# Second pair of k and q loaded in f32 on the hardware queues and turned sooner; last eviction in one copy

## The chip, the core and the metric

The kernel runs on one core of a Trainium2 chip. Its engines are TensorE (PE; its weight loads are listed as PEld), VectorE (DVE), ScalarE (ACT), GpSimd (POOL) and SyncE (SP). SyncE, ScalarE and GpSimd also issue DMA transfers; those of GpSimd can change the type on the way (f32 to bf16), those of SyncE and ScalarE here copy without a change of type. The metric is the device time of one execution in microseconds, and smaller is better.

## The reference

Two stages follow each other: attention with a soft cap on the scores, then a feed-forward layer whose hidden value is the larger of two products.

```
q, k, v: (8, 12, 448, 64) f32, cap = 30
scores = (q @ k^T) / 8
scores = cap * tanh(scores / cap)
attn   = softmax(scores)
x      = (attn @ v), heads side by side: (3584, 768)
out    = max(x @ w1, x @ w2) @ w_out        w1, w2: (768, 1024), w_out: (1024, 768)
```

The output has 3584 rows of 768 f32 values.

## The kernel before, in words

The heads are taken two at a time, as 48 pairs (`i`), and the pairs two at a time, as 24 units of four heads (`t`); a unit at a time goes through the attention (unit 2 is cut into two items of 256 and 192 queries, so the items `n` in the steps count to 25). The feed-forward layer is rewritten: `max(a, b) = relu(a - b) + b`, so that `out = relu(x (w1 - w2)) w_out + x (w2 w_out)`. The product `w2 w_out` is made once (`premultiply`), stage 1 makes `relu(x (w1 - w2))` and stage 2 sums both products into an output tile of 128 rows. All of this is cut into numbered groups of matmuls (140 of them), which run between the attention's matmuls.

The order is written out by hand, as the string `ORDER`: each step names a function and its arguments, and each engine executes its instructions in the order in which the steps give them. Nothing is rearranged later. The engines meet through semaphores: an instruction waits only for the data and the buffers that it needs. GpSimd's loads also share eight completion slots in turn, so a load waits for the one eight before it; the stores and loads of SyncE and ScalarE do the same among themselves.

The steps that matter here:

- `ld0 x` (`load_first`, L254): loads k or q of pair 0 in f32 into a tile of its own, k on SyncE's queue, q on ScalarE's. `cd x` (`cast_first`, L259) casts it to bf16 into `kqs`, k on VectorE, q on ScalarE.
- `lk i`, `lq i` (`load`, L272): k or q of pair i, cast on the way, on GpSimd's queue (L276). `lv`, `lw1`, `lw2`, `lwo` load v and the weights on the same queue.
- `dm`, `ms0`, `id`, `ms`: fill a dummy tile, the identity and the constants. `D bank n` (L331): n dummy matmuls of 128 columns that compute nothing that is used.
- `X i bank` (L356): 28 transposes on TensorE that turn k and q of pair i, of 64 by 64 each, into a PSUM bank; `Xh i c bank` does only k (c = 0) or only q (c = 1), 14 of them. `XC` (L366) copies them on VectorE to `qkT`.
- `S n s z` (L428): scores of part s of item n into PSUM slot z (0 or 1). `T n s` (L439): tanh on ScalarE, which reads the slot and so frees it. `L`, `TL` are the same for the last 64 keys (L448, L459). `E` (L463): the exponential on ScalarE.
- `W`, `WC`: turn w2 on TensorE and copy it. `O`, `M x y n`, `H`, `ev`: open a group, run n of its matmuls (L581; a single group in turn L576), hand the bank over, evict it. Groups 138 and 139 are the two column halves of the last output tile.

`stage2` (L632) evicts an output tile by half. For the last tile of the last batch it stores each half at once: the first half with one copy on VectorE (L650) and two stores, rows 0 to 63 on SyncE's queue (L651) and rows 64 to 127 on ScalarE's (L652); the second half with two copies, VectorE's for the first 64 rows (L655) and ScalarE's for the others (L656), which writes into the f32 tile that had held k of pair 0 (`kr` in the profile), and then the two stores (L657, L658).

The first steps are, in the order before:

```
ld0 q; dm; ms0; D 0 32; cd q; ld0 k; cd k; lq 3 0; id; Xh 0 1 0; XC 0 1; Xh 0 0 1; XC 0 0; ms; S 0 2 0; T 0 2;
S 0 0 1; T 0 0; S 0 1 0; T 0 1; E 0 0 0 3; lk 1 0; lq 1 0; lq 2 0; X 1 2; XC 1; S 0 3 1; S 0 4 0; T 0 4; T 0 3;
E 0 1 0 2; lk 2 0; X 2 3; lk 3 0; lv 0 2; X 3 0; XC 2; D 1 8; XC 3; S 1 4 0; T 1 4; S 1 5 1; T 1 5; lw2 0; W 0 1;
```

Of the kernel before, what the change touches and what calls it, by code (L numbers as in the profile page):

```python
# [6 lines left out]


ORDER = """
ld0 q; dm; ms0; D 0 32; cd q; ld0 k; cd k; lq 3 0; id; Xh 0 1 0; XC 0 1; Xh 0 0 1; XC 0 0; ms; S 0 2 0; T 0 2;  # L10
S 0 0 1; T 0 0; S 0 1 0; T 0 1; E 0 0 0 3; lk 1 0; lq 1 0; lq 2 0; X 1 2; XC 1; S 0 3 1; S 0 4 0; T 0 4; T 0 3;
E 0 1 0 2; lk 2 0; X 2 3; lk 3 0; lv 0 2; X 3 0; XC 2; D 1 8; XC 3; S 1 4 0; T 1 4; S 1 5 1; T 1 5; lw2 0; W 0 1;
W 1 2; WC 1; L 0 0; TL 0; S 0 5 1; T 0 5; D 3 8; L 1 0; TL 1; WC 0; lwo 0 0; O 0 3; O 1 0; M 0 1 4; S 1 2 1; T 1 2;
lk 4 0; lwo 0 1; M 0 1 3; S 1 3 0; T 1 3; M 0 1 1; H 0; H 1; M 1 0 1; E 0 1 2 4; M 1 0 3; S 1 1 1; T 1 1; S 1 0 0;
# [149 lines left out]
def kernel(  # L164
# [11 lines left out]
    nc = tc.nc  # L176
    f32 = mybir.dt.float32
    bf16 = mybir.dt.bfloat16
# [3 lines left out]
    B, H, S, D = q.shape  # L182
    assert (H, S, D) == (12, 448, 64) and B % 2 == 0
    DM = H * D
    DF = moe_w1.shape[1]
    P = 128
    KC, FC = DM // P, DF // P
# [5 lines left out]
    VB = 4  # L193
    QB = 3
    NS = 3
    W2T = 6
    WOP = 2
    R7 = S // 64
    OB = 4
    CUT = 256  # L200
    SPLIT = (2,)
    scale = 1.0 / (D ** 0.5)

    ctx.enter_context(tc.manual_schedule())
    const = ctx.enter_context(tc.tile_pool(name="const", bufs=1))
    stage = ctx.enter_context(tc.tile_pool(name="stage", bufs=2))
    att = ctx.enter_context(tc.tile_pool(name="att", bufs=2))
# [13 lines left out]
    warm = const.tile([P, P], bf16, name="warm")  # L221
# [8 lines left out]
    def rows_of(i):  # L230
        return kqs[i // 2 % KB].rearrange("p j c -> p (j c)")[:, (i % 2) * 2 * S : (i % 2 + 1) * 2 * S]
# [19 lines left out]
    raw = {}  # L251
    SRC = {"k": k, "q": q, "v": v}

    def load_first(what):  # L254
        raw[what] = stage.tile([P, S], f32, name=what + "r", bufs=1)
        eng = nc.sync if what == "k" else nc.scalar
        eng.dma_start(out=raw[what], in_=rows7(SRC[what], 0))

    def cast_first(what):  # L259
        if what == "k":  # L260
            nc.vector.tensor_copy(rows_of(0)[:, :S], raw[what])
        else:
            nc.scalar.copy(rows_of(0)[:, S:], raw[what])

    def rows7(t, i):
        b, p = divmod(i, NP)
        return t[b, 2 * p : 2 * p + 2, :, :].rearrange("h (r j) d -> (h r) (j d)", j=R7)
# [77 lines left out]
    def keep_w2(c):  # L345
        w2T[c] = stage.tile([P, FC * P], bf16, name="w2T", bufs=W2T)
        nc.vector.tensor_copy(w2T[c], turned[c])
# [41 lines left out]
    def heads(t):  # L389
        return [divmod(m, 2) if turned_by_pe(t) else divmod(m, 2)[::-1] for m in range(4)]  # L390


    ITEMS = [
        (t, c0, w) for t in range(N // 2) for c0, w in (((0, CUT), (CUT, S - CUT)) if t in SPLIT else ((0, S),))
    ]

    def cut(n):
        return ITEMS[n][2] < S

    exps = {}  # L400
    slots = {}

    def exps_of(n, o):
        key = (n, 1 if cut(n) else o)
        if key not in exps:
            if key[1]:
                exps[key] = att.tile([P, 8 * S], bf16, name="e1")
            else:
                exps[key] = att.tile([P, 6 * S], bf16, name="e0")
        return exps[key]  # L410

    def e_of(n, o, h, j):
        w = ITEMS[n][2]
        if cut(n):
            x = 4 * (o if j < 2 else 2) + 2 * h + (j if j < 2 else o)
        else:
            x = 2 * j + h
        return exps_of(n, o)[:, x * w : (x + 1) * w]

    def left_of(n):  # L420
        w = ITEMS[n][2]
        b = 12 if cut(n) else 6
        return exps_of(n, 1)[:, b * w : (b + 2) * w].rearrange("p (o s) -> p o s", o=2)
# [15 lines left out]
    def tanh(n, s):  # L439
        w = ITEMS[n][2]  # L440
        if cut(n):
            e, m, x = exps_of(n, 1), 2 * w, s
        else:
            e, m, x = exps_of(n, s // NJ), w, s % NJ
        e = e[:, 2 * x * m : 2 * (x + 1) * m].rearrange("p (h s) -> p h s", h=2)
        nc.scalar.activation(e, slots[n, s][:, :, :m], AF.Tanh, scale=scale / cap)  # L446
# [42 lines left out]
    def total(n, bank):  # L489
        t, c0, w = ITEMS[n]  # L490
        ss = sums[n] = mm_tile(bank)
        HR = list(zip(heads(t), R32))
        if t < NS:
            for j in range(NJ):
# [108 lines left out]
    def stage1(b, f, c0, w):  # L603
        cs = slice((b % 2) * S + c0, (b % 2) * S + c0 + w)

        def unit(c):
            return wd_sb[:, c, f * P : (f + 1) * P], xT[b // 2][:, c, cs]

        def done(ps):
            if b // 2 not in gT:  # L610
                gT[b // 2] = xpool.tile([P, FC, 2 * S], bf16, name="gT", bufs=1)
            nc.vector.tensor_relu(gT[b // 2][:, f, cs], ps)  # L612

        return Group(KC, w, unit, done)
# [15 lines left out]
    osbs = {}  # L630

    def stage2(b, t, half):  # L632
        hs = slice(half * (DM // 2), (half + 1) * (DM // 2))
        ts = slice(t * P, (t + 1) * P)

        def unit(c):
            if c < KC:
                return xT[b // 2][:, c, ts], wm_sb[:, c, hs]
            return gT[b // 2][:, c - KC, ts], wo_sb[:, c - KC, hs]

        def done(ps):
            if (b, t) not in osbs:
                osbs[b, t] = osb_all[:, (7 * (b // 2) + t) % OB, :DM]
            o = osbs[b, t]
            if (b, t) != (B - 1, 6):
                nc.vector.tensor_copy(o[:, hs], ps)  # L646
                return
            to = out[b * S : (b + 1) * S, :].rearrange("(r j) n -> j r n", j=R7)[R7 - 2 :]
            if half == 0:
                nc.vector.tensor_copy(o[:, hs], ps)  # L650
                nc.sync.dma_start(out=to[0][:, hs], in_=o[:64, hs])  # L651
                nc.scalar.dma_start(out=to[1][:, hs], in_=o[64:, hs])  # L652
                return
            o2 = raw["k"][64:, : DM // 2]
            nc.vector.tensor_copy(o[:64, hs], ps[:64])  # L655
            nc.scalar.copy(o2, ps[64:])  # L656
            nc.sync.dma_start(out=to[0][:, hs], in_=o[:64, hs])  # L657
            nc.scalar.dma_start(out=to[1][:, hs], in_=o2)  # L658

        return Group(KC + FC, DM // 2, unit, done)  # L660

    groups = {}

    def number(new):
        for g in new:
            groups[len(groups)] = g

    number(premultiply(c, half) for half in range(2) for c in range(KC))
    for b in range(B):
        if b == 0 and SPLIT:  # L670
            number(stage1(b, f, 0, CUT) for f in range(FC))
            number(stage2(b, t, half) for t in range(CUT // P) for half in range(2))
            number(stage1(b, f, CUT, S - CUT) for f in range(FC))
            number(stage2(b, t, half) for t in range(CUT // P, 3) for half in range(2))
        else:
            number(stage1(b, f, 0, S) for f in range(FC))
            number(stage2(b, t, half) for t in (range(3) if b % 2 == 0 else range(3, 7)) for half in range(2))
# [4 lines left out]
    def moe(x, y, n):  # L682
# [6 lines left out]
                    groups[g].step(h)  # L689

    STEPS = {
        "ld0": load_first, "cd": cast_first, "ms": fill_const, "dm": lambda: nc.vector.memset(warm, 0.0),
        "ms0": lambda: nc.vector.memset(ident, 0.0), "id": identity, "D": keep_warm,
        "lk": lambda i, x: load("k", i, x), "lq": lambda i, x: load("q", i, x), "lv": load_v,
        "lw1": load_w1, "lw2": load_w2, "lwo": load_wo, "cr": cross,
# [45 lines left out]
```

## Time and profile before

| | |
|---|---|
| time, median of 3 runs | 329.57 us (329.55 to 329.63) |
| the profiled execution's own time | 329.6 us |
| its span in the profile | 327.8 us |
| TensorE busy | 318.9 us, 97% of the span |
| ScalarE busy | 273.8 us, 84% |
| VectorE busy | 244.8 us, 75% |
| GpSimd busy (mostly issuing loads) | 164.2 us, 50% |

A line of the timeline has the start in us, the busy time, the engine, the line of the kernel, the operation with output and input, the count, and in brackets how long the engine was idle before it and what it waited for. SPq and ACTq are the queues of SyncE and ScalarE as they issue transfers. The chain is the work that ended last, followed back from the last instruction to what released it. A busy TensorE is not TensorE at its peak: the ends of its matmuls are modelled.

### The profile page before, as it was taken

Reading aid. Unit: us, or ns where it says so; the run is one execution under the profiler, and the core shown is the slowest. Engines: PE = TensorE matmul, PEld = TensorE weight load, DVE = VectorE, ACT = ScalarE, POOL = GpSimd, SP = SyncE. Lnnn points to the kernel's source line nnn. Section 1 sums busy time; section 2 is a strip of 40 time slices with the busy share of each in tenths; the row PEclk is TensorE's granted clock in tenths of the full one; section 3 lists DMA queues with packets and bytes.
Section 4 is the critical chain, followed back from the end, with each engine's and each line's share of the span. In section 5 each row is a group of like instructions: output and inputs, shape, how many; then the busy total and the mean of one; then the engine's idle time right before and its main releaser. Section 6 shows DMA issues by size and latency. Waiting matters only on the chain.

```text
span 327.8 us, 10012 instructions
## 1 busy us (share of the span) xinstructions
PE 318.9 (97%) x4288; PEld 195.6 (60%) x4288; DVE 244.8 (75%) x446; ACT 273.8 (84%) x245; POOL 164.2 (50%) x243
## 2 busy tenths in 40 slices
PE   6899999999999999999999999999999999999994
PEld 5555567576556655655665565675567667655562
DVE  2339799889877887987888778878789775995421
ACT  4998999999999999999999998999899988710000
POOL 8447488988885994776567386543202000000000
PEclk9599999999999999999999999999999999999999
DMA  8999999999999999999999999995953042004006
GB/s 147 192 176 239 261 217 144 150 178 144 170 179 187 150 138 139 189 187 197 152 169 157 134 150 200 182 77 95 194 118 46 2 115 79 3 2 144 2 0 192
DMA packets 135083, 45.90 MB, mean 140 GB/s; under 512 B 116224, under 2 KB 130816, under 8 KB 134656
## 3 DMA queue, kind: packets, MB, share of 16 engines
q0 software_dynamic: 95456, 25.08, 75.8%
q1 hardware_dynamic: 39040, 19.18, 30.1%
q10 hardware_dynamic: 544, 1.02, 0.9%
q8 instruction: 33, 0.54, 0.7%
q14 instruction: 10, 0.08, 0.1%
HBM read 47.45 MB, written 11.01 MB: 178 GB/s over the span
## 4 chain that ended last, share of the span: by engine, by line
PE 88%; ACT 8%; DMA 1%; issue 1%; DVE 0%; DVEq 0%
PE mm L581 56%; PE s L538 8%; PE mm L576 8%; PE s L437 8%; ACT e L446 5%; ACT e L468 3%; PE s L528 2%; PE s L455 2%; PE mm L501 1%; DMA qr<-in_q_dram 1%; PE mm L364 1%; PE mm L496 1%; PE mm L343 1%; ACT e L461 0%; DVE qkT L369 0%
## 5 line engine op out<-in xcount | busy, mean ns | idle before, releaser
L468 ACT ACTIVATE e<-e 128x1792 bf16<-128x1792 bf16 (+4 forms) x73 | 140.7, 1937 | 0.3
L446 ACT ACTIVATE e<-s 128x896 bf16<-128x896 f32 (+2 forms) x144 | 123.8, 933 | 10.7 <-PE s L437 10.7
L581 PE MATMUL mm<-wo_sb,gT 64*128 64x384 bf16 x768 | 96.3, 323 | 0.0
L581 PE MATMUL mm<-xT,wd_sb 64*128 64x448 bf16 (+2 forms) x768 | 80.1, 326 | 0.0
L581 PE MATMUL mm<-wm_sb,xT 64*128 64x384 bf16 x576 | 77.2, 323 | 0.0
L283 POOL DMA_DIRECT2D kqs<-in_k_dram x76 | 54.5, 720 | 17.7 <-DMA kqs<-in_q_dram 7.7
L581 PEld LDWEIGHTS <-gT 64*128 64x128 bf16 x768 | 49.0, 94 | 22.6 <-issue 2.3
L581 PEld LDWEIGHTS <-wd_sb 64*128 64x128 bf16 x768 | 46.7, 94 | 19.8 <-issue 2.9
L437 PE MATMUL s<-qkT 64*128 64x448 bf16 (+2 forms) x300 | 53.9, 349 | 2.6 <-DVE qkT L369 1.3
L301 POOL DMA_DIRECT2D vp<-in_v_dram x48 | 30.4, 638 | 47.2 <-PE mm L501 28.2
L581 PEld LDWEIGHTS <-xT 64*128 64x128 bf16 x576 | 38.9, 94 | 16.6 <-issue 2.2
L612 DVE TENSOR_SCALAR gT<-mm 128x448 bf16<-128x448 f32 (+2 forms) x72 | 39.2, 567 | 10.2 <-PE mm L581 5.5
L646 DVE COPY osb<-mm 128x384 f32<-128x384 f32 x54 | 29.2, 552 | 19.3 <-PE mm L576 10.4
L283 POOL DMA_DIRECT2D kqs<-in_q_dram x38 | 34.9, 919 | 6.8 <-DMA kqs<-in_k_dram 3.9
L538 PE MATMUL s<-e,vp 128*32 128x448 bf16 (+2 forms) x600 | 32.5, 347 | 0.0
L557 DVE TENSOR_TENSOR xT<-s,inv 64x448 bf16<-64x448 f32 (+2 forms) x50 | 30.2, 603 | 2.2 <-PE mm L581 1.2
L301 POOL DMA_DIRECT2D vl<-in_v_dram x48 | 29.3, 619 | 4.0 <-DMA gT<-in_moe_w_dram 3.0
L437 PEld LDWEIGHTS <-qkT 64*128 64x128 bf16 x300 | 20.8, 94 | 17.4 <-issue 4.8
L656 ACT COPY kr<-mm 64x384 f32<-64x384 f32 x1 | 0.5, 473 | 36.0 <-DVE osb L655 36.0
L478 DVE TENSOR_TENSOR esum<-e 128x896 bf16<-128x896 bf16 x42 | 25.6, 616 | 5.0 <-PE mm L581 2.7
L483 DVE TENSOR_TENSOR esum<-esum,e 64x896 bf16<-64x896 bf16 x42 | 26.0, 618 | 3.1 <-PE mm L581 1.4
L478 DVE TENSOR_TENSOR esum<-esum,e 128x896 bf16<-128x896 bf16 x42 | 25.5, 622 | 3.1 <-PE mm L581 1.3
(56 smaller groups left out, 278.1 us busy)
## 6 DMA issues: line engine op xcount, KB each, us to landing
out_dram<-osb SPq DMA_DIRECT2D x51, 192.0 KB, 4.3
vp<-in_v_dram POOLq DMA_DIRECT2D x38, 160.0 KB, 5.1
kqs<-in_q_dram POOLq DMA_DIRECT2D x47, 112.0 KB, 5.5
kqs<-in_k_dram POOLq DMA_DIRECT2D x76, 56.0 KB, 4.8
osb<-in_moe_w_dram POOLq DMA_DIRECT2D x2, 1024.0 KB, 8.4
gT<-in_moe_w_dram POOLq DMA_DIRECT2D x3, 512.0 KB, 10.0
wo_sb<-in_moe_w_out_dram POOLq DMA_DIRECT2D x4, 384.0 KB, 8.6
w1l<-in_moe_w_dram POOLq DMA_DIRECT2D x1, 1024.0 KB, 6.1
```

The lines of the kernel that those rows point to most:

```text
L283: nc.gpsimd.dma_start(out=to, in_=x)
L301: nc.gpsimd.dma_start(out=to, in_=x)
L437: nc.tensor.matmul(ps[:, h, x * w : (x + 1) * w], k_of(t, o, h, j), q_of(n, o, h))
L446: nc.scalar.activation(e, slots[n, s][:, :, :m], AF.Tanh, scale=scale / cap)
L468: nc.scalar.activation(e[:, j0 * m : hi], e[:, j0 * m : hi], AF.Exp, scale=float(cap))
L478: nc.vector.tensor_add(d, e[:, 0:2, :] if j == 1 else d, e[:, 2 * j : 2 * j + 2, :])
L538: nc.tensor.matmul(vals[n][R32[m], u, :w], vp[t % VB][:, x, j if turned_by_pe(t) else 2 * j, u::2], e_of(n, o, h, j), start=False, stop=(j ...
L557: nc.vector.tensor_mul(x[to], vals[n][r, 1, :w], sums[n, 3][to, :w])
L576: nc.tensor.matmul(self.ps, w, x, start=first, stop=self.at[0] == self.n)
L581: ins = nc.tensor.matmul(self.ps, w[r], x[r], start=first, stop=self.at == [self.n, self.n]).ins
L612: nc.vector.tensor_relu(gT[b // 2][:, f, cs], ps)
L646: nc.vector.tensor_copy(o[:, hs], ps)
```

## The change

K and q of pair 1 are loaded as those of pair 0 were: in f32, k on SyncE's queue and q on ScalarE's, each behind pair 0's, and cast by VectorE (k) and ScalarE (q). GpSimd's queue has these two loads no more, and the loads behind them move up. Of pair 0, k is turned and copied before q, where it was q before k. The transposes of pair 1 move ahead of the third scores of item 0. In the last tile the second half is evicted as the first: one copy of 128 rows on VectorE, and two stores from the same tile. Three names are added that keep the sizes as they were: `EB = 2` (buffers of the exponentials, two before as well), `LASTW = 384` (columns of the last tile's first half, 384 before as well) and the width of a stage 2 group that follows from it.

```diff
 ORDER = """
-ld0 q; dm; ms0; D 0 32; cd q; ld0 k; cd k; lq 3 0; id; Xh 0 1 0; XC 0 1; Xh 0 0 1; XC 0 0; ms; S 0 2 0; T 0 2;
-S 0 0 1; T 0 0; S 0 1 0; T 0 1; E 0 0 0 3; lk 1 0; lq 1 0; lq 2 0; X 1 2; XC 1; S 0 3 1; S 0 4 0; T 0 4; T 0 3;
+ld0 k; ld0 q; ld1 k; ld1 q; dm; ms0; D 0 32; cd k; cd q; cd1 q; lq 3 0; id; Xh 0 0 1; XC 0 0; Xh 0 1 0; XC 0 1; cd1 k;
+ms; S 0 2 0; T 0 2; S 0 0 1; T 0 0; X 1 2; S 0 1 0; T 0 1; E 0 0 0 3; lq 2 0; XC 1; S 0 3 1; S 0 4 0; T 0 4; T 0 3;
...
-    def load_first(what):
-        raw[what] = stage.tile([P, S], f32, name=what + "r", bufs=1)
+    def load_first(what, i=0):
+        raw[what, i] = stage.tile([P, S], f32, name=f"{what}r{i}", bufs=1)
         eng = nc.sync if what == "k" else nc.scalar
-        eng.dma_start(out=raw[what], in_=rows7(SRC[what], 0))
+        eng.dma_start(out=raw[what, i], in_=rows7(SRC[what], i))
-    def cast_first(what):
+    def cast_first(what, i=0):
         if what == "k":
-            nc.vector.tensor_copy(rows_of(0)[:, :S], raw[what])
+            nc.vector.tensor_copy(rows_of(i)[:, :S], raw[what, i])
         else:
-            nc.scalar.copy(rows_of(0)[:, S:], raw[what])
+            nc.scalar.copy(rows_of(i)[:, S:], raw[what, i])
...
-                exps[key] = att.tile([P, 8 * S], bf16, name="e1")
+                exps[key] = att.tile([P, 8 * S], bf16, name="e1", bufs=EB)
...
-        hs = slice(half * (DM // 2), (half + 1) * (DM // 2))
+        w = LASTW if (b, t) == (B - 1, 6) else DM // 2
+        hs = slice(w, DM) if half else slice(0, w)
...
-            if half == 0:
-                nc.vector.tensor_copy(o[:, hs], ps)
-                nc.sync.dma_start(out=to[0][:, hs], in_=o[:64, hs])
-                nc.scalar.dma_start(out=to[1][:, hs], in_=o[64:, hs])
-                return
-            o2 = raw["k"][64:, : DM // 2]
-            nc.vector.tensor_copy(o[:64, hs], ps[:64])
-            nc.scalar.copy(o2, ps[64:])
+            nc.vector.tensor_copy(o[:, hs], ps)
             nc.sync.dma_start(out=to[0][:, hs], in_=o[:64, hs])
-            nc.scalar.dma_start(out=to[1][:, hs], in_=o2)
+            nc.scalar.dma_start(out=to[1][:, hs], in_=o[64:, hs])
...
+        "ld1": lambda w: load_first(w, 1), "cd1": lambda w: cast_first(w, 1),
```

More of the change, by code (lines that the diff above doesn't have):

```diff
@@ L195 @@
     NS = 3
+    EB = 2
     W2T = 6
@@ L201 @@
     SPLIT = (2,)
+    LASTW = 384
     scale = 1.0 / (D ** 0.5)
@@ L406, in exps_of @@
             if key[1]:
-                exps[key] = att.tile([P, 8 * S], bf16, name="e1")
+                exps[key] = att.tile([P, 8 * S], bf16, name="e1", bufs=EB)
             else:
-                exps[key] = att.tile([P, 6 * S], bf16, name="e0")
+                exps[key] = att.tile([P, 6 * S], bf16, name="e0", bufs=EB)
         return exps[key]
@@ L648, in done @@
             to = out[b * S : (b + 1) * S, :].rearrange("(r j) n -> j r n", j=R7)[R7 - 2 :]
-            if half == 0:
-                nc.vector.tensor_copy(o[:, hs], ps)
-                nc.sync.dma_start(out=to[0][:, hs], in_=o[:64, hs])
-                nc.scalar.dma_start(out=to[1][:, hs], in_=o[64:, hs])
-                return
-            o2 = raw["k"][64:, : DM // 2]
-            nc.vector.tensor_copy(o[:64, hs], ps[:64])
-            nc.scalar.copy(o2, ps[64:])
+            nc.vector.tensor_copy(o[:, hs], ps)
             nc.sync.dma_start(out=to[0][:, hs], in_=o[:64, hs])
-            nc.scalar.dma_start(out=to[1][:, hs], in_=o2)
-        return Group(KC + FC, DM // 2, unit, done)
+            nc.scalar.dma_start(out=to[1][:, hs], in_=o[64:, hs])
+        return Group(KC + FC, hs.stop - hs.start, unit, done)
     groups = {}
@@ L691 @@
     STEPS = {
-        "ld0": load_first, "cd": cast_first, "ms": fill_const, "dm": lambda: nc.vector.memset(warm, 0.0),
+        "ld0": load_first, "cd": cast_first, "ld1": lambda w: load_first(w, 1), "cd1": lambda w: cast_first(w, 1), "ms": fill_const, "dm": lambda: nc.vector.memset(warm, 0.0),
         "ms0": lambda: nc.vector.memset(ident, 0.0), "id": identity, "D": keep_warm,
```

## The prediction

> **What bounds the kernel now.** I read the page first, then the chain that ended last in order of time, then the timeline of the head and of the tail, then the clock by stretches. A row of the chain or the timeline gives start us, length us and what; a bracket gives the idle time before the row and what ended it.
>
> ```profile
> span 327.8 us, 10012 instructions
> ...
> PE 318.9 (97%) x4288; PEld 195.6 (60%) x4288; DVE 244.8 (75%) x446; ACT 273.8 (84%) x245; POOL 164.2 (50%) x243
> ...
> PEclk9599999999999999999999999999999999999999
> ...
> PE 88%; ACT 8%; DMA 1%; issue 1%; DVE 0%; DVEq 0%
> ```
>
> TensorE is the bound of the whole, with no slack to speak of, but the diff touches only the first 10 us and the last 5. There the chain is this:
>
> ```profile
> 0.74 3.56 DMA qr<-in_q_dram
> ...
> 4.33 0.57 ACT kqs L263
> ...
> 4.94 0.43 PE mm L364 x14
> ...
> 5.39 0.70 DVE qkT L369 x2
> ...
> 6.14 0.38 PE s L437 x2
> ...
> 6.54 2.54 ACT e L446 x3
> ...
> 14.89 1.62 ACT e L446 x2
> ...
> 16.55 0.37 PE s L437 x2
> 16.92 0.55 PE mm L335 x8
> ```
>
> Up to 6.54 us it is one string: q lands, ScalarE casts, TensorE turns q and k, VectorE copies both, the first scores, the first tanh (T 0 2). From 6.54 to 16.51 the chain stays on ScalarE without a gap, so TensorE's work in these 10 us is hidden. From 16.55 on it is TensorE's. So the head is worth what it moves the start of T 0 2, now 6.54. If TensorE falls behind before 16.55 it costs nothing, and after that everything.
>
> **The change part by part.** The head by its rows:
>
> ```profile
> 0.74 0.41 SPq L257 DMA_DIRECT2D kr<-in_k_dram  x1
> ...
> 1.17 1.28 ACT L263 ACT_TABLE_LOAD   x1 [1.17 <-PEq L722]
> 1.24 0.68 POOL L276 DMA_DIRECT2D kqs<-in_q_dram  x1 [0.79 <-POOLq L722]
> ...
> 2.79 1.09 POOL L276 DMA_DIRECT2D kqs<-in_q_dram  x2
> ...
> 4.16 0.47 DVE L261 CAST kqs<-kr 128x448 bf16<-128x448 f32 x1 [3.15 <-DMA kr<-in_k_dram]
> ...
> 4.94 0.63 PE L364 MATMUL mm<-ident,kqs 64*64 64x64 bf16 x28 [0.36 <-ACT kqs L263]
> ...
> 6.14 0.55 PE L437 MATMUL s<-qkT 64*128 64x448 bf16 x4 [0.57 <-DVE qkT L369]
> ...
> 7.51 0.37 PE L437 MATMUL s<-qkT 64*128 64x448 bf16 x2 [0.82 <-ACT e L446]
> ...
> 9.34 0.93 PE L437 MATMUL s<-qkT 64*128 64x448 bf16 x4 [0.73 <-DVE qkT L369]
> ```
>
> *K before q.* k's cast ends at 4.63, but its turning waits behind q's, whose cast ends at 4.90. In the new order k is turned from 4.67 (4.63 and the 0.04 seen between cast and turning). Its 14 transposes show at 5.10 (0.43), VectorE's copy runs 5.12 to 5.47 (half of 0.70). q is turned meanwhile, from about 4.99, its rows showing by 5.4, and its copy follows at 5.47 to 5.82. The first scores come at 5.87 instead of 6.14, and T 0 2 at 6.27 to 6.28: a gain of 0.26. q may land 0.1 later than now before this is touched.
>
> *The second issue on SyncE and ScalarE.* One costs 0.41. On ScalarE it pushes the table load from 1.17 to 1.57; that ends at 2.85, well before the cast at 4.33: nothing. SyncE has nothing else to do.
>
> *Two loads fewer on GpSimd's queue.* An issue is 0.55 (half of 1.09), so every later load is issued about 1.1 us sooner. The bytes read are the same. I price it at nothing, because TensorE waits for no transfer after the head; this is the whole list of what it waited for from 17 us to the end:
>
> ```profile
> PE mm L581 <- DVEq L589: 0.2, 1, 0.2
> ```
>
> *The casts of pair 1.* ScalarE's (the like one took 0.57) stands in front of T 0 2, VectorE's (0.47) behind the two copies. ScalarE is free from 4.90 to 6.28, so its cast costs nothing if q of pair 1 lands by 5.68. It costs the whole gain if it lands at 5.94, and beyond that each 0.1 costs 0.1. When it lands no row shows. These bound it:
>
> ```profile
> kr<-in_k_dram SPq DMA_DIRECT2D x1, 224.0 KB, 3.4
> qr<-in_q_dram ACTq DMA_DIRECT2D x1, 224.0 KB, 3.6
> ...
> 2.80:3.40 0.60, 1.00 1.06 409
> 3.40:4.40 1.00, 1.00 1.26 218
> ```
>
> (Landing in us after issue; then a stretch, its length, the clock, the share of the DMA engines, GB/s.) While the first pair's 458 KB moved, the engines gave 409 GB/s, so the second pair needs another 1.12 us behind q's landing at 4.30: 5.42 at the soonest. If GpSimd's transfers, the mixed 218 GB/s of the later stretch, take a third of the engines it is 4.30 + 1.68 = 5.98. Both ends stay in the range: a gain of 0.26, or a loss of 0.04. I take a landing of at most 5.68, since the 409 is nearer: the two hardware queues had the engines to themselves although GpSimd's first load was already issued at 1.24. The Trainium skill ("DMA: Bandwidth & Descriptors", Queues, rings and completion order) has each DMA engine go round between the queues that have work, a packet at a time. By that rule the third queue does take its third, the landing is 5.98 and the head is worth nothing; the row of 409 doesn't decide it, since it doesn't show when GpSimd's descriptors were ready.
>
> VectorE's cast delays the constants' fills (0.4) and the copy of pair 1's transposes. The constants are read only by the sums of the first unit, far behind. The copy now has no wait left that ScalarE would feel, as below.
>
> *Pair 1 turned sooner.* Its 28 transposes (0.63) move in front of the third scores, into the 0.82 in which TensorE waited for ScalarE: from 6.45 to 7.1, while the slot comes free at about 7.2. The wait of 0.73 at 9.34 goes. What is late next is ScalarE, which reads those scores only after the exponential that ends at 11.55. So nothing is gained, and nothing lost unless the k and q casts end after about 6.6.
>
> *The tail.* Column limits stay at 384 and the exponent buffers at two, so EB and LASTW change nothing. What changes is the last eviction:
>
> ```profile
> 323.63 0.55 DVE L655 COPY osb<-mm 64x384 f32<-64x384 f32 x1 [1.72 <-PE mm L576]
> 324.21 0.47 SPq L657 DMA_DIRECT2D out_dram<-osb  x1
> 324.22 0.47 ACT L656 COPY kr<-mm 64x384 f32<-64x384 f32 x1 [36.03 <-DVE osb L655]
> 324.72 0.47 ACTq L658 DMA_DIRECT2D out_dram<-kr  x1
> ...
> out_dram<-osb SPq DMA_DIRECT2D x1, 96.0 KB, 2.2
> out_dram<-kr ACTq DMA_DIRECT2D x1, 96.0 KB, 2.1
> ...
> L646 DVE COPY osb<-mm x54: 518/557/559, 68.1 to 319.6; 128x384 f32<-128x384 f32 x54
> ```
>
> The two copies are meant to be side by side but ran one behind the other: ScalarE's was released by VectorE's. 128 rows take VectorE 0.557, as long as 64 (0.55). So both stores can be issued at 324.22. ScalarE's landed at 324.72 + 2.1 = 326.8; like SyncE's it would at 324.22 + 2.2 = 326.4: a gain of 0.4. The ends are 0.2 (both writes queue behind 326.4, their bytes still to move) and 0.5 (the whole move of the issue).
>
> Sum, against the profiled execution's own 329.6 (span 327.8 and 1.8 around it; the median of three, 329.57, is the same): 329.6 - 0.26 - 0.40 = 328.94, so **328.9**. What a measurement of this kernel can tell from no change is about 0.2%, 0.66 us: this forecast lies at that line.
>
> **The rivals.** The clock is the one that ends on the other side. These are stretches of 3.41 us between the two changes of the clock (length, TensorE's busy us and matmuls, clock, DMA, GB/s), and one group of dummy matmuls at each clock:
>
> ```profile
> 4.65:8.06 3.41, 1.73 (x50) 1.00 1.20 165
> 8.06:11.48 3.42, 2.69 (x76) 0.50 1.06 175
> 11.48:14.89 3.41, 3.41 (x40) 0.50 1.28 197
> 14.89:18.30 3.41, 2.56 (x41) 1.00 1.18 212
> ...
> 11.83 1.04 PE L335 MATMUL mm<-warm 128*128 128x128 bf16 x8
> ...
> 16.85 0.62 PE L335 MATMUL mm<-warm 128*128 128x128 bf16 x8
> ```
>
> The clock halved after a stretch that was 51% busy, stayed half after 79%, came back after 100% and stayed full after 75%. In the trace of before the half clock lies wholly under ScalarE and is free. The change moves 0.63 of transposes from behind 8.06 to before it (about 65% busy then), and all turning after it comes sooner, so the stretch 11.48 to 14.89 loses work: with a full clock it keeps four scores and the turning of w2, some 1.7 us, half of it. *Rival 1*: the clock halves at 14.89, where TensorE becomes the bound. The eight dummies cost 0.42 more, the scores before them 0.19 (half of 0.93 less half of 0.55, rounded), the left scores behind them about 0.26 (the dummies' ratio of 1.68 on 0.38): 0.9, so 329.8, if the clock is back at 18.3. If the stretch to 18.3 is again not busy enough, another 3.41 us run slow. These lose 1.4 (by the ratio 1.68) to 1.7 (by 0.5), say 1.5: 331.3. For it: the 51% row. Against it: if the clock halves at 8.06 as now, the slow matmuls themselves fill the stretches. It decides as soon as the half clock reaches past 16.5. The Trainium skill ("TensorE: Matmul & The Clock Gate", The HAM clock gate) describes such a gate, judged in free-running windows of 3413 ns; the 6.83 between the two changes here is two of them, so the trace agrees on the length, and the page names no share at which it halves.
>
> *Rival 2*: pair 1's q lands late, at 5.98 to 6.3. ScalarE's cast then holds T 0 2 to 6.58 to 6.9, so the head loses 0.04 to 0.36 and the tail's 0.4 stays: 329.2 to 329.6.
>
> *Rival 3*: the head's shift doesn't arrive, or the tail's doesn't, because something not seen takes it up: one gain of 0.26 or 0.4 alone gives 329.2 to 329.3.
>
> **How the numbers follow.** The forecast with its ends (328.5 to 329.2) has 52 in 100; I put 39 of them below 328.91, since the soonest landing and the tail's whole 0.5 both are near rows. Rivals 2 and 3 have 16 together, all within 0.2%. Rival 1 has 32: 13 for the short form (within 0.2%, 6 of them beyond through a longer tail of slow matmuls) and 19 for the long one. So faster 0.39, within 0.2% 0.36 (13 + 16 + 7), slower 0.25 (19 + 6). The range 328.4 to 331.0 leaves out most of the long form of rival 1 and little below; the likeliest case's own range is 328.5 to 329.2.
>
> **What would show it.** In the changed trace: T 0 2 at about 6.28, with pair 1's q cast ended before it; the chain still on ScalarE from there to about 16.3; pair 1 turned before 7.2 with no wait at the scores that follow; the last two stores both issued 0.6 after the last matmul and landed 0.4 sooner. I am wrong in the head if T 0 2 begins behind a cast that waited for its load, in the free cover if the clock is 0.5 at 15 to 18 us with TensorE's first long groups later than 17.8, and in the tail if the last landing keeps its distance of 3.2 from the last matmul.

## The result, and the profile after

The changed kernel takes 331.45 us (median of 22 runs, 329.82 to 332.38) against 329.72 for the kernel before (22 runs, 329.34 to 331.94): a ratio of 1.0041, 95% interval 1.0027 to 1.0055. It is slower by 1.7 us where 0.7 less was forecast. The spread is part of the result: 19 of the 22 runs lie above 330.5, of the kernel before 3 of 22.

The profiled execution took 331.03 (span 329.2). Its chain in order of time, by the new line numbers (L337 dummies, L366 transposes, L371 their copies, L439 scores, L457 the scores of the last keys, L583 groups of matmuls):

```profile
4.59 0.53 PE mm L366 x10
5.14 0.78 DVE qkT L371 x2
5.96 0.38 PE s L439 x2
6.36 2.54 ACT e L448 x3
8.93 2.44 ACT e L470
11.37 1.62 ACT e L448 x2
13.02 1.70 ACT e L470
14.71 1.62 ACT e L448 x2
16.38 0.56 PE s L439 x2
16.93 0.96 PE mm L337 x8
17.90 0.50 PE s L457 x8
18.40 1.29 PE mm L583 x8
19.69 0.19 PE s L439 x2
19.88 0.49 PE mm L583 x5
20.37 0.19 PE s L439 x2
20.56 0.21 PE mm L583 x2
20.78 0.09 issue
20.95 0.83 PE mm L583 x8
```

Up to 16.38 everything is as forecast in kind: T 0 2 starts at 6.36 instead of 6.54, the chain stays on ScalarE, and it leaves it 0.17 sooner (16.38 for 16.55). Then the eight dummies take 0.96 instead of 0.55 and the first group of eight matmuls 1.29 instead of 0.76. The group that starts at 20.95 started at 19.80 before: 1.15 later, and this lag is still there at the end, where the last matmul ends at 324.75 instead of 323.59, 1.16 later.

TensorE in the stretches of 3.41 us that lie between the changes of its clock (length, busy us and matmuls, clock, DMA, GB/s):

```profile
5.81:9.22 3.41, 2.11 (x38) 1.00 1.17 142
9.22:12.64 3.42, 2.02 (x68) 1.00 1.13 190
12.64:16.05 3.41, 1.75 (x26) 1.00 1.32 208
16.05:19.46 3.41, 3.08 (x26) 0.50 1.21 197
19.46:22.88 3.42, 3.19 (x44) 1.00 1.21 204
```

The clock no longer halves at 8.06. TensorE is 62% and then 59% busy and keeps it; in the third stretch it is 51% busy, the clock halves at 16.05 and comes back at 19.46. Before, the half clock lay from 8.06 to 14.89, under ScalarE. Now it lies on the first 3 us in which TensorE is the bound.

### The profile page after: what moved, and what is told of

It reads as the page before. It is cut to its first block, busy times and chain, and to the rows that moved or that the text cites. A ratio compares the mean times of both kernels' runs of the same rounds, so it can differ in the third digit from the quotient of the medians.

```text
span 329.2 us, 10016 instructions
## 1 busy us (share of the span) xinstructions
PE 318.3 (97%) x4288; PEld 195.3 (59%) x4288; DVE 245.1 (74%) x447; ACT 274.1 (83%) x245; POOL 163.1 (50%) x241
## 4 chain that ended last, share of the span: by engine, by line
PE 89%; ACT 8%; issue 1%; DVE 0%; DVEq 0%
PE mm L583 56%; PE s L540 8%; PE mm L578 8%; PE s L439 8%; ACT e L448 5%; ACT e L470 3%; PE s L457 2%; PE s L530 2%; PE mm L337 1%; PE mm L503 1%; PE mm L366 1%; PE mm L498 1%; PE mm L345 1%; ACT e L463 0%; DVE qkT L371 0%
## 5 line engine op out<-in xcount | busy, mean ns | idle before, releaser
L448 ACT ACTIVATE e<-s 128x896 bf16<-128x896 f32 (+2 forms) x144 | 123.7, 935 | 10.2 <-PE s L439 10.1
L583 PE MATMUL mm<-wo_sb,gT 64*128 64x384 bf16 x768 | 96.4, 323 | 0.0
L583 PE MATMUL mm<-xT,wd_sb 64*128 64x448 bf16 (+2 forms) x768 | 80.0, 326 | 0.0
L583 PE MATMUL mm<-wm_sb,xT 64*128 64x384 bf16 x576 | 77.3, 323 | 0.0
L583 PEld LDWEIGHTS <-gT 64*128 64x128 bf16 x768 | 49.0, 94 | 22.4 <-issue 2.3
L583 PEld LDWEIGHTS <-wd_sb 64*128 64x128 bf16 x768 | 46.9, 94 | 19.4 <-issue 2.7
L439 PE MATMUL s<-qkT 64*128 64x448 bf16 (+2 forms) x300 | 53.3, 344 | 3.9 <-ACT e L448 3.4
L583 PEld LDWEIGHTS <-xT 64*128 64x128 bf16 x576 | 38.9, 94 | 16.6 <-issue 2.2
L439 PEld LDWEIGHTS <-qkT 64*128 64x128 bf16 x300 | 21.1, 94 | 18.7 <-issue 7.3
L463 ACT ACTIVATE e<-s 128x896 bf16<-128x896 f32 (+2 forms) x25 | 22.5, 899 | 1.3 <-PE s L457 1.0
```

Of the source, the lines that this page charges most:

```text
L439: nc.tensor.matmul(ps[:, h, x * w : (x + 1) * w], k_of(t, o, h, j), q_of(n, o, h))
L583: ins = nc.tensor.matmul(self.ps, w[r], x[r], start=first, stop=self.at == [self.n, self.n]).ins
```

## The experiments

Two theories stood against each other: that the loss is the place of the half clock, and that something else in the change costs (the loads on the hardware queues, the casts in front of T 0 2, or the tail). Each run was timed beside the kernel before on the same chip; "high" counts the runs above 330.5, the kernel before's in the same set behind it.

| run | median us (range) | kernel before | ratio, 95% interval | high |
|---|---|---|---|---|
| e1_tail_only | 329.96 (329.56 to 332.18) | 329.64 | 1.0010 (0.9997 to 1.0024) | 1 of 12; 1 of 29 |
| e2_head_only | 331.69 (329.99 to 332.10) | 329.64 | 1.0047 (1.0030 to 1.0064) | 5 of 6; 1 of 29 |
| e3_fill | 329.65 (329.45 to 331.59) | 329.64 | 1.0004 (0.9993 to 1.0015) | 1 of 11; 1 of 29 |
| e4_sooner_only | 331.81 (329.64 to 332.32) | 329.64 | 1.0048 (1.0030 to 1.0066) | 8 of 12; 1 of 29 |
| e5_fill_oldtail | 329.92 (329.70 to 330.95) | 329.76 | 1.0000 (0.9984 to 1.0016) | 2 of 12; 3 of 35 |
| e6_fill_lastw512 | 329.49 (329.18 to 329.80) | 329.76 | 0.9979 (0.9960 to 0.9997) | 0 of 12; 3 of 35 |
| e7_fill_late | 329.92 (329.58 to 332.20) | 329.76 | 1.0006 (0.9986 to 1.0025) | 3 of 12; 3 of 35 |
| e8_x_back | 329.94 (329.65 to 332.30) | 329.76 | 1.0009 (0.9987 to 1.0030) | 2 of 12; 3 of 35 |
| e9_before_w512 | 329.48 (329.19 to 329.73) | 329.64 | 0.9985 (0.9971 to 1.0000) | 0 of 12; 3 of 29 |
| e10_kfirst | 329.74 (329.37 to 331.81) | 329.64 | 1.0002 (0.9986 to 1.0018) | 1 of 12; 3 of 29 |
| e11_kfirst_w512 | 329.53 (329.25 to 330.85) | 329.64 | 0.9990 (0.9973 to 1.0007) | 1 of 12; 3 of 29 |
| e12_thin | 331.96 (331.34 to 332.22) | 329.64 | 1.0059 (1.0036 to 1.0082) | 6 of 6; 3 of 29 |

### Head and tail apart

Run e1 takes the tail alone. In the kernel before, the branch of the second half is dropped:

```diff
-            if half == 0:
-                nc.vector.tensor_copy(o[:, hs], ps)
...
-            o2 = raw["k"][64:, : DM // 2]
-            nc.vector.tensor_copy(o[:64, hs], ps[:64])
-            nc.scalar.copy(o2, ps[64:])
+            nc.vector.tensor_copy(o[:, hs], ps)
             nc.sync.dma_start(out=to[0][:, hs], in_=o[:64, hs])
-            nc.scalar.dma_start(out=to[1][:, hs], in_=o2)
+            nc.scalar.dma_start(out=to[1][:, hs], in_=o[64:, hs])
```

> The kernel before with the tail of the changed one alone (one copy of 128 rows, two stores from one tile), head as before. Tail as predicted (the last landing follows the last issue by 2.1 to 2.2): 0.4 us below the kernel before, about 329.3. The changed trace speaks for another size: there the stores were issued 0.51 sooner after the last matmul but landed 2.5 and 2.7 after issue, so the theory that the queued writes set the end expects 0.0 to +0.25: 329.7 to 329.9. The clock theory (the loss is in the head) expects no run like the 332 of the changed kernel beyond those that the kernel before has too.

It gave no gain: 329.96 against 329.64, with an interval that holds 1. Run e2 is the opposite, the changed kernel with the old tail put back (the same lines the other way, `raw["k", 0]` for `raw["k"]`):

> The changed kernel with the old tail (two copies, ScalarE's into the f32 tile). Clock theory, loss in the head: 331.0 to 331.5, spread from 329.8 to 332.4 as in the changed kernel. If the tail made the loss: 329.5, 0.2 below the kernel before.

331.69 against 329.64: the loss is all in the head.

### The cause in the head

Run e4 moves nothing but the transposes of pair 1, in the kernel before; loads, casts, k and q of pair 0 and the tail stay:

```diff
-S 0 0 1; T 0 0; S 0 1 0; T 0 1; E 0 0 0 3; lk 1 0; lq 1 0; lq 2 0; X 1 2; XC 1;
+S 0 0 1; T 0 0; lk 1 0; lq 1 0; lq 2 0; X 1 2; S 0 1 0; T 0 1; E 0 0 0 3; XC 1;
```

> The kernel before with the transposes of pair 1 ahead of the third scores, all loads and casts as before, old tail. Clock theory: TensorE's work in the first 15 us moves forward and thins out the stretch before 15 us as in the changed kernel, so 330.5 to 331.5 with a wide spread. If it is the loads on the hardware queues or the casts that cost: 329.7 as before.

This alone makes the whole loss (331.81). Run e8 is its counterpart: the changed head (with the old tail) with these transposes put back.

```diff
-X 1 2; S 0 1 0; T 0 1; E 0 0 0 3; lq 2 0; XC 1;
+S 0 1 0; T 0 1; E 0 0 0 3; lq 2 0; X 1 2; XC 1;
```

> The changed head and the old tail, but pair 1's transposes put back behind the third scores; loads, casts and k before q as changed. Clock theory: TensorE still gets ahead of ScalarE (the loads land in time, nothing waits), so part of the loss stays: 330 to 331.5, spread wide. If only the place of these transposes makes it: 329.4 to 329.7, like the kernel before less the 0.18 of the head.

329.94 against 329.76, 2 runs of 12 high: the loss is gone within what this can tell. My own expectation for it under the clock theory, that a part would stay, was too high. So loads, casts and k before q cost nothing that shows, and the place of 28 transposes does. That it acts through the clock is shown by filling TensorE's idle time in the changed kernel, without putting the transposes back:

```diff
-D 1 8; XC 3; S 1 4 0; T 1 4; S 1 5 1;
+D 1 24; XC 3; S 1 4 0; T 1 4; D 1 6; S 1 5 1;
...
-W 1 2; WC 1;
+W 1 2; D 3 14; WC 1;
```

> The changed kernel with dummy matmuls in TensorE's idle stretches between 10.8 and 15.5 us (16 more, 6 and 14 of 128 columns, in cover of ScalarE). Clock theory: the clock stays full from 14 to 20 us, the runs draw together and the median falls to 329.3 to 329.8 (0.18 sooner in T 0 2, nothing from the tail). If the loss lies in the loads, the casts or the tail: 331.4 as the changed kernel, or slower by what the dummies cost.

36 dummy matmuls more, and the time falls from 331.45 to 329.65. TensorE from 10 to 23 us in the changed kernel, then filled, then in e4:

```profile
10.00:14.00 4.00, 2.20 (x45) 1.00 1.22 195
14.00:17.00 3.00, 1.41 (x20) 0.84 1.27 216
17.00:20.00 3.00, 3.00 (x30) 0.59 1.28 200
20.00:23.00 3.00, 2.77 (x46) 1.00 1.18 195
```

```profile
10.00:14.00 4.00, 3.34 (x62) 1.00 1.18 184
14.00:17.00 3.00, 2.46 (x42) 1.00 1.25 214
17.00:20.00 3.00, 2.77 (x40) 1.00 1.27 201
20.00:23.00 3.00, 3.00 (x65) 1.00 1.19 194
```

```profile
10.00:14.00 4.00, 2.20 (x58) 1.00 1.22 195
14.00:17.00 3.00, 1.60 (x22) 0.67 1.24 215
17.00:20.00 3.00, 3.00 (x28) 0.50 1.28 199
20.00:23.00 3.00, 2.77 (x24) 0.69 1.21 197
```

The filled kernel keeps 1.00 throughout and gets 40 matmuls done between 17 and 20 us, where the changed one gets 30 and e4 28; between 20 and 23 it is 65, 46 and 24. In e4 the half clock lasts two stretches of 3.41 us, and its last matmul ends at 326.07, 2.48 after the kernel before's.

Run e12 goes the other way: the changed head with the old tail, and the eight dummies that both kernels have at 10 us left out.

```diff
-XC 2; D 1 8; XC 3;
+XC 2; XC 3;
```

> The changed head with the old tail, and the eight dummy matmuls that both kernels have at 10 us left out: TensorE's stretch before 15 us is thinner still. Clock theory: the fall comes in nearly every run, the median rises to 331.7 to 332.2 and no run is near 329.8. If the clock is not it: 331.5 or a little less, since work is taken away.

Less work, and slower: 331.96, with all six runs high. The stretches around the fall in its trace, cut at its own changes of the clock:

```profile
4.51:7.92 3.41, 2.24 (x63) 1.00 1.27 194
7.92:11.33 3.41, 1.73 (x60) 1.00 0.97 160
11.33:14.75 3.42, 2.46 (x18) 0.50 1.28 198
14.75:18.16 3.41, 3.02 (x33) 0.50 1.19 211
```

Here it halves after a stretch at 51%, stays half through 72% and 89%, and is back only at 21.57. In the first 30 us of the traces of both kernels and all runs, cut in the same way at the changes that the clock column shows, it halved after stretches that were 47 to 57% busy and stayed full after 56% or more; once half, it stayed so after 65 to 89% and came back after 90 to 100%. These are busy shares as the profile models them, and the first two ranges touch, so they give no sharp limit.

Run e7 fills only the hole behind the turning of w2 (`D 3 14`, old tail):

> The changed head, old tail, and only the last group of the dummies (14, behind the turning of w2, in the idle stretch before 15.5 us). Clock theory: whether the clock falls depends on where its stretch of 3.4 us begins, so one idle hole filled helps a part of the runs: between 329.5 and 331.5, with both levels among the runs. If the hole behind the turning of w2 alone makes the fall: 329.4, all together.

329.92, three of 12 high, the highest 332.20. Most of the cure is in that one hole, just before the bound passes to TensorE, but not all of the risk.

### The gains that were forecast

Run e10 turns k of pair 0 before q in the kernel before, and nothing else:

```diff
-Xh 0 1 0; XC 0 1; Xh 0 0 1; XC 0 0;
+Xh 0 0 1; XC 0 0; Xh 0 1 0; XC 0 1;
```

> The kernel before with one edit: k of pair 0 turned and copied before q. The head's term of the forecast alone: T 0 2 sooner by 0.2 and the time lower by 0.2, with no loss by the clock, since pair 1's transposes stay where they were. If the clock takes this too (TensorE a little further ahead of ScalarE): no gain, and some runs near 332.

In its profile T 0 2 starts at 6.29, but the median doesn't move (329.74 against 329.64). Run e5, the filled kernel with the old tail, says the same:

> The filled kernel (dummy matmuls in the idle stretches of the changed head) with the old tail of two copies. Clock theory plus a tail that gave nothing or lost a little: the head's 0.18 is left as a gain, 329.3 to 329.5, with the runs drawn together; this would be below both kernels. If the tail is neutral: 329.65 as the filled kernel.

329.92 against 329.76, ratio 1.0000. In its profiled run, 330.85 and one of two near 331, the dummies that cover idle time took time themselves; the chain there is TensorE's from 9.53 to 17.23, the dummies in it. The rows of the timeline:

```profile
6.21 0.93 PE L439 MATMUL s<-qkT 64*128 64x448 bf16 x4 [0.49 <-DVE qkT L371]
...
10.01 1.70 PE L366 MATMUL mm<-ident,kqs 64*64 64x64 bf16 x56
11.65 2.41 PE L337 MATMUL mm<-warm 128*128 128x128 bf16 x24
```

These are the times of the half clock (0.93 and 1.70 as at half clock before), in a run whose clock column shows 1.00 there: the column shows a change only from the first one recorded.

Run e6 cuts the last tile of the filled kernel at 512 columns (`LASTW = 512`), so that the last two stores carry 64 KB instead of 96:

> The filled kernel with the last tile cut at 512 columns in place of 384 (one copy per part): the last two stores move 64 KB each in place of 96. If queued bytes set the end of the tail, the last landing comes 0.1 to 0.2 sooner after the last matmul: 329.4 to 329.55. If the issue sets it: 329.65, unchanged.

329.49 against 329.76, the first ratio wholly below 1 (0.9960 to 0.9997). Run e9 does it with the head of the kernel before (one copy per part, `w = 512` for the last tile), e11 adds k first:

> The kernel before, head untouched, with the last tile cut at 512 columns and one copy per part. If the queued bytes set the end, as the cut gave in the filled kernel: 0.15 to 0.3 below the kernel before. If that gain was the head's: no change.

> Both: k first, and the last tile cut at 512. If the two gains add: 0.35 to 0.5 below the kernel before, the best of all. If either is not there: 0.2 below.

329.48 and 329.53 against 329.64. The cut gives 0.16 without any change in the head, at the edge of its interval (0.9971 to 1.0000); k first adds nothing that shows. So e9 and e6 are below both kernels, by little, and e9 is the simpler one.

## Why the prediction was wrong, point by point

*The step that failed: "Pair 1 turned sooner", which the sum puts at nothing ("nothing gained, and nothing lost").* Run e4 makes this one edit and loses 2.2 in the median (331.81 against 329.64); in the traced run of the changed kernel the loss is 1.15. The mechanism was named, as rival 1: the clock halves where TensorE becomes the bound, after a stretch that is half busy. It came so, at 16.05 after a stretch at 51%. But it was given 32 in 100, and 19 of 22 runs lie above 330.5, with the traced one that shows the late half clock (331.03); where it lay in the others is not on record. The argument against it, that slow matmuls fill the stretches if the clock halves at 8.06 as now, fell with its premise, and the prediction's own figure spoke against that premise: the stretch before 8.06 would be about 65% busy. It is 66% in e4 (4.80 to 8.22), and the clock stays full there; the transposes took the halving away from a place where it was free.

I also reasoned with the stretches of one trace, as if they began at the same time in every run. They don't. The kernel before, e1 and e9 have the same steps in the head, and their clocks halve at 8.06, 9.18 and 7.31; the changed kernel and e2 have the same head, and theirs halve at 16.05 and 14.60. So it isn't one stretch that must stay busy, but every stretch whose half clock can reach past 16.5, wherever it begins. The Trainium skill ("TensorE: Matmul & The Clock Gate", The HAM clock gate) says that the window is free-running and doesn't reset when the kernel starts; these five traces bear that out, and I had cited the sentence only for its length.

*The prices of rival 1.* The short form was put at 0.9 and measured 1.33 (1.15 late at the group of 20.95, and T 0 2 0.18 sooner): the first group of eight matmuls, 0.53 slower, was missing from the sum. The long form was put at 2.4, and e4 comes out 2.48 late, 0.08 of it a later T 0 2. That this agrees is partly luck: 2.4 was 0.9 and 1.5, and the 0.9 was too small.

*The sum's ends* were not worked out right either: 329.6 less 0.26 and less 0.2 to 0.5 gives 328.84 to 329.14, and 329.44 with the late landing, not 328.5 to 329.2. And 39 of the 52 chances were put below 328.91, though the forecast itself was 328.94.

*The head's 0.26* was 0.18 in the profile of the changed kernel. What was overlooked is TensorE's pace in the first 6 us. K was cast at 4.42, sooner than the 4.63 of the sum, but the 32 dummies, which run from 0.99 for 3.60, held TensorE until 4.59. The 28 transposes behind them took 0.95, where they took 0.63 before, so VectorE's copies began at 5.14 and took 0.78 (5.12 and 0.70 in the sum). In the timeline of the changed head:

```profile
0.99 3.60 PE L337 MATMUL mm<-warm 128*128 128x128 bf16 x32 [0.99 <-DVE warm L688]
...
4.03 0.39 DVE L263 CAST kqs<-kr 128x448 bf16<-128x448 f32 x1 [3.02 <-DMA kr<-in_k_dram]
...
4.52 0.95 PE L366 MATMUL mm<-ident,kqs 64*64 64x64 bf16 x28
...
5.30 0.56 ACT L265 CAST kqs<-qr 128x448 bf16<-128x448 f32 x1 [0.52 <-DMA qr<-in_q_dram]
...
6.45 0.63 PE L366 MATMUL mm<-ident,kqs 64*64 64x64 bf16 x28
```

What the sum says of T 0 2, that its shift carries through to the end, holds in the profiles: in the six that have the last tile cut at 384 and the chain on ScalarE, with a full clock behind it (the kernel before, e1, e3, e7, e8, e10), the last matmul ends 317.04 to 317.12 after T 0 2 starts. In the changed kernel it is 318.39, in e2, e4 and e12, with the longer half clock, 319.34 to 319.48: the price of the half clock once more, about 1.3 and 2.3 to 2.4. Yet the gain is in no median (e5, e8, e10, e11), and why not stays open. T 0 2 itself moves as much from run to run: 6.54, 6.62 and 6.48 in three profiles with q turned first and 6.80 in a fourth, in which the transposes took 0.95; with k first it starts at 6.17 to 6.38 in nine and at 6.81 in e5, where TensorE was slow longer.

*The casts and loads* were right: pair 1's q had landed by 5.30, sooner than the soonest I allowed (5.42), and its cast ended at 5.86, before T 0 2 could start. The rule of "DMA: Bandwidth & Descriptors" (Queues, rings and completion order) in the Trainium skill, read as a third of the engines for GpSimd's queue, would have given 5.98; the trace doesn't agree with that reading. Rival 2 did not occur.

*Pair 1 turned sooner* did what was said, in the hole that was said (6.45 to 7.08), and "nothing gained, nothing lost" was the wrong price for it: moved to where it hides better, it moved the half clock from under ScalarE to where TensorE is the bound.

*The tail's 0.4* was nothing. The stores were both issued 0.63 after the last matmul, as forecast, and landed later after issue:

```profile
325.38 0.47 SPq L653 DMA_DIRECT2D out_dram<-osb  x1
325.38 0.50 ACTq L654 DMA_DIRECT2D out_dram<-osb  x1
...
out_dram<-osb SPq DMA_DIRECT2D x1, 96.0 KB, 2.5
out_dram<-osb ACTq DMA_DIRECT2D x1, 96.0 KB, 2.7
```

2.7 instead of 2.1: the last landing is 3.33 after the last matmul, where it was 3.23. The step that failed here took the landing of a store as a length of its own. From the issue at 325.38 to the last landing the engines moved 594 KB (220 GB/s for 2.70), and these two stores are 197 of them: the engines were still moving what had been queued. That is the lower end that I had named, and its 0.2 was still too much. What moved the end is the cut at 512, with smaller last stores (the rows are e6's, e9's are the same):

```profile
out_dram<-osb SPq DMA_DIRECT2D x1, 64.0 KB, 2.4
out_dram<-osb ACTq DMA_DIRECT2D x1, 64.0 KB, 2.6
```

with a last copy of 0.42 in place of 0.56. In e9 the last landing is 3.09 after the last matmul, 0.24 sooner than in the changed kernel: 0.14 by the shorter copy and 0.10 by the time from issue to landing. No run separates the two.

## What to carry to other kernels

Work that is hidden under another engine may still be paying for TensorE's clock. Before moving it to a better-hidden place, add up TensorE's busy time in every window of the length that the trace shows (3.41 us here) up to the point where TensorE becomes the bound, wherever the window begins, and look for one near half. A half clock that lay early, under ScalarE, was free here; the one that fell later cost 1.3 to 2.4 us. A few dummy matmuls in the hole just before the hand-over are a cheap test of it (331.45 to 329.65 here). When the last bytes are queued behind others, an earlier issue doesn't move the end (e1); a smaller last piece did, by 0.16, at the edge of what could be told (e9).

## What was not expected of the hardware

The place of the clock's stretches differs between executions, also where the heads are the same (8.06, 9.18 and 7.31 above), so one change shows as a spread and not as a shift: the changed kernel ran from 329.82 to 332.38, and without the eight dummies at 10 us every run was above 331.3. The clock needs far more to come back than to stay: 89% of a stretch at half clock did not bring it back (e12), 56% at full clock kept it (e1).
